# Blocks 14 and 15 of an interleaved down product, put back for two chunks of a four-layer prompt kernel

## The chip, the cores and the metric

The kernel runs on one core of a Trainium2 chip. The metric is the device time of one execution in microseconds (us). The engines are named as in the profile: PE is TensorE (PEld are its weight loads), DVE is VectorE, ACT is ScalarE, POOL is GpSimd, SP is SyncE, whose queue issues the transfers.

## The reference, cut to what matters

Two kinds of layers alternate, A, B, A, B, on x of 2048 tokens by 576 features. A is a dilated sliding-window attention (32 heads of 18 features, 8 keys at distance 0, 2, ... 14), B a gated product without an activation function. The same weights serve both A layers, and the same both B layers.

```python
x = x + A(layernorm(x), wqkv, wo)
x = x + B(layernorm(x), w_gate, w_up, w_down)
x = x + A(layernorm(x), wqkv, wo)
x = x + B(layernorm(x), w_gate, w_up, w_down)
...
def B(x, w_gate, w_up, w_down):   # w_gate, w_up: 576 x 4608, w_down: 4608 x 576
    h = (x @ w_gate) * (x @ w_up)
    return h @ w_down
```

The change lies in the last product, h @ w_down, of the first B layer.

## The kernel before, in words

**Tiles.** Tokens go in tiles of 128, so 2048 tokens are 16 tiles. The 4608 inner features of B are 36 feature tiles of 128 (`NFT`). The 576 outer features are four full row tiles and a tail of 64.

**Units and down blocks.** B is computed in units and blocks. A unit (`g_unit`, L1038) multiplies the normalised tokens with some feature tiles of w_gate and w_up into two PSUM banks: four full row tiles at L1046, the tail of 64 rows at L1056. Then ScalarE copies both banks out (L1000, L1002) and VectorE multiplies the two copies (L1003), which leaves h for these feature tiles in a buffer. Units are issued in batches (`batch`, L1014), so that the tails of several units run together. The down product (`Down`, L1065) accumulates h @ w_down over blocks. A block (`block`, L1091) takes `blk` feature tiles (2 here) for each token tile: for every pair of token tile and feature tile it loads h as weights and streams 512 columns of w_down (L1106), then loads it again for the last 64 columns (L1107). With 36 feature tiles there are 18 blocks. The first and last matmul of an accumulation are marked for the first and last block. `close` (L1118) adds the accumulators to the residual (L1123, L1133).

**Rows of w_down.** They come in pairs of feature tiles into a ring of six buffers wd (`load_wd`, L988). `fetch` (L1074) is called with each block and stays ahead of it by the length of the ring; it asks for all 18 pairs in order, whichever blocks are called.

**Stages.** The first 1024 tokens of the first B layer go through small stages, in which the weights are still arriving and attention of later chunks runs beside the matmuls: `first_pair` for two tiles, then `small` (L1240) three times for chunks of 256 tokens (entries 2, 3 and 4 of `seq`). Entry 2 runs all units and then all blocks. Entries 3 and 4, the third and fourth chunk, run with `inter` set: a unit has two feature tiles, there are 18 units (`nu`), and they share four buffers in hb in turn (`homes`, 14 + u % 4). So blocks must run between the units. In every second unit from u = 4 on, L1260 to L1262 run blocks u - 4 and u - 3, which read the units of these numbers. The loop ends at u = 17, so the last pair in it is blocks 12 and 13 at u = 16. The blocks left over come at L1265, behind the last batch (units 16 and 17). In the kernel before this second loop begins at `nu - 2` = 16, so blocks 14 and 15, feature tiles 28 to 31, are not added for these 512 tokens. After the small stages six large ones (`big`, L1270) take 512 tokens each, with units for one feature tile and 512 tokens.

**Order.** Every operation is recorded in a plan (`Plan`, L21) with a cost, its reads and writes, and a priority. `run` (L72) then issues greedily what can start first by its own clocks of the engines, the transfers and the free PSUM banks. Units and blocks hang on a chain in their own order (`bb`, L981); attention work (scores L744 to L754, softmax L785 to L852, values L912 and L928, output product L951, residual L957) and the transposes of the normalised input (L453, by transfers) are placed between them by the plan, some with a margin. Each engine runs its list in the order that the plan wrote, as does SP's queue.

Of the kernel before, what the change touches and what calls it, by code (L numbers as in the profile page):

```python
# [141 lines left out]
def kernel(  # L142
# [26 lines left out]
    NFT = F // P  # L169
# [347 lines left out]
    def place(la, t0, nst):  # L517
        b, o = order_sc.index((la, t0 // NSC)) % 2, t0 % NSC
        return xnT_B[b][:, :, o * P:(o + nst) * P], [f"xB{b}_{o + i}" for i in range(nst)]
# [518 lines left out]
    def g_unit(fts, xT, xk, n, dst, dk, act):  # L1038
        use, keys = [{}, {}], [f"{nm}_{dk}" for nm in ("wg", "wu")]

        def full(first, last_):
            for q, (nm, views) in enumerate((("wg", wgv), ("wu", wuv))):
                def fn(ws=[wcol(views, ft) for ft in fts], q=q):
                    for e, w_ in enumerate(ws):
                        for k in range(KF):
                            nc.tensor.matmul(ring[use[q]["slot"]][:, e * n:(e + 1) * n], lhsT=w_[:, k], rhs=xT[:, k],  # L1046
                                             start=(first and k == 0 and e == 0), stop=(last_ and k == KF - 1), skip_group_check=True)
                kw = dict(hold="ring", use=use[q]) if first else {}
                bb("PE", len(fts) * KF * (n / 2.4 + (1.8 if n < 256 else 2.9)), fn, r=xk + fkeys(nm, fts), w=[keys[q]], **kw)

        wt = [wcol(wtv, ft) for ft in fts]

        def tails(fresh):
            for e, w_ in enumerate(wt):
                for q, r_ in enumerate((slice(0, TL), slice(TL, 2 * TL))):
                    nc.tensor.matmul(ring[use[q]["slot"]][:, e * n:(e + 1) * n], lhsT=w_[r_], rhs=xT[r_, KF], start=(fresh and e == 0),  # L1056
                                     stop=not fresh, skip_group_check=True)

        def evac():
            fg, fu = [dict(free="ring", use=x) for x in use]  # L1060
            evacuate(lambda p_: ring[use[p_]["slot"]], keys, dst, dk, SC, act, fg, fu)
        return dict(use=use, keys=keys, full=full, tails=tails, npairs=len(fts), slotns=n * 0.42, evac=evac,
                    rk=xk + fkeys("wgt", fts) + fkeys("wut", fts), done=[])
# [82 lines left out]
    def pusher(size, opens=2):  # L1146
        bat = []

        def push(u=None, mid=None):
            if u is not None:  # L1150
                bat.append(u)
            if bat and (u is None or len(bat) == size):
                us = list(bat)
                bat.clear()
                batch(us, mid, opens)
        return push
# [9 lines left out]
    def hand_over(pool_k, slots):  # L1166
        for uses in slots:
            got, outs = {}, []

            def fn(got=got, outs=outs, uses=uses):  # L1170
                for p_, o_ in enumerate(outs):
                    o_.use["slot"] = 7 - got["slot"] if pool_k == "pa" else got["slot"] * uses + p_ + (4 if pool_k == "boot" else 0)
                    if pool_k == "boot" and o_.use["slot"] == 6:
                        o_.use["slot"], o_.free = 1, "pa"
            chain["pe"] = op("PE", 0, fn, prio=1, after=chain["pe"], hold=pool_k, use=got)
            for _ in range(uses):
                outs.append(op("PE", 0, lambda: None, prio=1, after=chain["pe"], free="ring", use={}))
                chain["pe"] = outs[-1]

    def begin_units(jobs, push):  # L1180
        for q in jobs:
            units = []
            begin(q, units)
            for x in units:
                push(x)

    def insert_d(jobs):
        for q in jobs:
            units = []
            begin(q, units)  # L1190
            while units:
                batch(units[:2])
                del units[:2]
# [46 lines left out]
    def small(j, inter, in_gu, in_d):  # L1240
        la, t0, nst = seq[j]
        n, fpu = nst * P, 4 // nst
        nu = NFT // fpu
        homes = [14 + u % 4 for u in range(nu)] if inter else [*range(9, 14), *range(9), *range(14, 18)]

        def lhs(ft, i):
            o = (ft % fpu) * n + i * P
            return hblk[homes[ft // fpu]][:, o:o + P]
        dn = Down(t0, nst, list(range(NFT)), lhs, lambda ft, i: f"hm{homes[ft // fpu]}", la == n_al - 1, False, 2)
        dn.fetch(len(wd_ring))  # L1250
        push = pusher(2, 1) if inter else pusher(3)
        marks["ld"], marks["ld1"] = marks.get("ld1"), chain["pe"]
        xT, xk = place(la, t0, nst)
        if j > 2:
            next(gens[j], None)
        if j == 3:
            hand_over("pa", (1,))
        for u in range(nu):
            begin_units(in_gu.get(u, ()), push)
            if inter and u % 2 == 0 and u > 2:  # L1260
                for b in (u - 4, u - 3):
                    dn.block(b)  # L1262
            push(g_unit(range(u * fpu, (u + 1) * fpu), xT, xk, n, hblk[homes[u]], f"hm{homes[u]}", True))
        push()
        for b in range(nu - 2 if inter else 0, NFT // 2):  # L1265
            insert_d(in_d.get(b, ()))
            dn.block(b)
        dn.close()
# [71 lines left out]
    for j in (2, 3, 4):  # L1340
        small(j, j > 2, IN_GU.get(j, {}), IN_D.get(j, {}))
# [38 lines left out]
```

## Time and profile before

| | |
|---|---|
| time, median of three runs | 1047.74 us |
| the three runs | 1047.56, 1047.74, 1049.56 us |
| the profiled execution, its own time | 1048.04 us |
| its span, first to last instruction | 1046.3 us |
| third chunk of 256 tokens: blocks 0 and 1 to blocks 16 and 17 | about 191 to 246 us |
| fourth chunk: the same | about 254 to 304 us |

The page gives busy time by engine, the span in slices, the chain that ended last, and groups of instructions by line; line numbers are those of the kernel before. A timeline row gives start, duration, engine, line, operation, output <- inputs, count, and in brackets the engine's idle time before it with the instruction that ended it. Matmuls overlap, since their recorded end is modelled; the distance of two starts is what one takes from the queue.

### The profile page before, as it was taken

The numbers are of one execution on the slowest core, as the hardware profiler recorded it, in microseconds if no ns is written. First come the engines' busy times: TensorE is split into PE (matmuls) and PEld (weight loads), VectorE is DVE, ScalarE is ACT, GpSimd is POOL, SyncE is SP. The second block draws the span as 40 slices with busy tenths as digits, with TensorE's granted clock in tenths as the row PEclk, the third lists the DMA queues.
The fourth block names the chain that finished last, engine by engine and source line by source line (L and its number), as shares of the span: only waits on it lengthen the run. The fifth ranks groups of instructions, "written<-read, shape, count | busy, mean of one in ns | idle before, by whom it ended". The sixth has DMA issues, their size and how long they took to land.

```text
span 1046.3 us, 19604 instructions
## 1 busy us (share of the span) xinstructions
PE 1028.7 (98%) x7898; PEld 598.7 (57%) x8016; DVE 723.7 (69%) x1366; ACT 446.3 (43%) x905; POOL 14.3 (1%) x54
## 2 busy tenths in 40 slices
PE   7999999999999999999999999999999999999998
PEld 6886886777765445554455544564455644554445
DVE  7896797879849886397776967579684696832211
ACT  5663763554645641354424443154431444214420
POOL 5000000000000000000000000000000000000000
PEclk9999999999999999999999999999999999999999
DMA  8928117445743705465143541625435252454212
GB/s 244 319 75 208 36 41 229 107 121 159 172 126 101 224 15 147 126 153 182 45 130 94 189 133 49 157 71 181 134 84 155 99 164 92 114 159 136 68 46 91
DMA packets 139850, 135.50 MB, mean 130 GB/s; under 512 B 43376, under 2 KB 137456, under 8 KB 139760
## 3 DMA queue, kind: packets, MB, share of 16 engines
q1 hardware_dynamic: 139760, 134.25, 44.2%
q8 instruction: 62, 1.02, 0.4%
q14 instruction: 28, 0.23, 0.1%
HBM read 114.49 MB, written 10.88 MB: 120 GB/s over the span
## 4 chain that ended last, share of the span: by engine, by line
PE 96%; issue 1%; DVE 1%; POOL 1%; DMA 1%; ACT 0%; POOLq 0%
PE pu L1046 20%; PE pg L1046 18%; PE pg L1106 8%; PE pu L1106 7%; PE acct L1046 6%; PE pg L551 5%; PE pa L1046 4%; PE pu L551 4%; PE acct L1106 3%; PE pu L1056 3%; PE pg L1056 3%; PE pg L1107 2%; PE pa L1106 2%; PE pu L1107 2%; PE pa L951 1%
## 5 line engine op out<-in xcount | busy, mean ns | idle before, releaser
L1046 PEld LDWEIGHTS <-reg 128*128 128x128 bf16 x3072 | 277.8, 98 | 222.3 <-issue 24.2
L1046 PE MATMUL pu<-xnT_B,reg 128*128 128x512 bf16 (+2 forms) x1302 | 231.4, 316 | 1.3 <-issue 0.3
L1046 PE MATMUL pg<-xnT_B,reg 128*128 128x512 bf16 (+2 forms) x1204 | 220.3, 319 | 1.0 <-issue 0.2
L1106 PEld LDWEIGHTS <-reg 128*128 128x128 bf16 x864 | 84.5, 98 | 98.2
L1000 ACT CAST g_sb<-pu 128x512 bf16<-128x512 f32 x112 | 65.6, 588 | 126.1 <-PE pg L1056 66.2
L1003 DVE TENSOR_TENSOR reg<-reg,g_sb 128x512 bf16<-128x512 bf16 x144 | 59.7, 419 | 86.0 <-ACT reg L1002 76.4
L551 PEld LDWEIGHTS <-wqkv 128*128 128x128 bf16 (+1 forms) x1050 | 88.2, 97 | 34.0 <-issue 18.2
L744 DVE TENSOR_TENSOR prod<-qT,kT 128x2560 bf16<-128x2560 bf16 (+1 forms) x68 | 96.4, 1420 | 8.2 <-ACT kT L671 7.1
L912 DVE TENSOR_TENSOR prod<-vT,ab 128x1280 bf16<-128x1280 bf16 (+1 forms) x120 | 92.1, 776 | 0.2 <-DMA ab<-a_dram 0.2
L1000 ACT CAST g_sb<-pg 128x512 bf16<-128x512 f32 x112 | 65.8, 589 | 60.8 <-PE pu L1056 30.1
L928 DVE TENSOR_TENSOR qT<-qT,prod 128x1280 bf16<-128x1280 bf16 (+1 forms) x112 | 89.7, 801 | 2.5
L1107 PEld LDWEIGHTS <-reg 128*128 128x128 bf16 x864 | 84.7, 98 | 1.8
L430 ACT ACTIVATE rstd<-mv,eps_t 128x2 f32<-128x2 f32 (+1 forms) x33 | 9.8, 297 | 162.8 <-DVE mv L426 159.9
L1046 PE MATMUL acct<-xnT_B,reg 128*128 128x512 bf16 (+1 forms) x303 | 69.4, 354 | 0.5 <-issue 0.3
L551 PE MATMUL pg<-xnT_A,wqkv 128*128 128x256 bf16 (+1 forms) x500 | 69.6, 273 | 0.0
L1056 PE MATMUL pu<-xnT_B,reg 64*128 64x512 bf16 (+2 forms) x331 | 67.6, 315 | 0.1
L1106 PE MATMUL pg<-wd,reg 128*128 128x512 bf16 (+1 forms) x232 | 63.9, 369 | 0.0
L1056 PE MATMUL pg<-xnT_B,reg 64*128 64x512 bf16 (+2 forms) x305 | 62.8, 318 | 0.0
L551 PE MATMUL pu<-xnT_A,wqkv 128*128 128x256 bf16 (+1 forms) x410 | 59.1, 273 | 0.1
L1106 PE MATMUL pu<-wd,reg 128*128 128x512 bf16 x200 | 54.8, 380 | 0.0
L1046 PE MATMUL pa<-xnT_B,reg 128*128 128x512 bf16 (+1 forms) x211 | 54.2, 375 | 0.6 <-issue 0.2
L1107 PE MATMUL pu<-wd,reg 128*128 128x64 bf16 x280 | 54.0, 193 | 0.8
(233 smaller groups left out, 1452.1 us busy)
## 6 DMA issues: line engine op xcount, KB each, us to landing
wd<-in_B_w_down_dram SPq DMA_DIRECT2D x152, 288.0 KB, 3.3
reg<-in_B_w_gate_dram SPq DMA_DIRECT2D x24, 768.0 KB, 4.7
reg<-in_B_w_up_dram SPq DMA_DIRECT2D x24, 768.0 KB, 6.3
reg<-in_B_w_down_dram SPq DMA_DIRECT2D x28, 288.0 KB, 3.3
s_dram<-s SPq DMA_DIRECT2D x13, 512.0 KB, 3.8
rg<-s_dram SPq DMA_DIRECT2D x52, 128.0 KB, 3.1
ab<-a_dram SPq DMA_DIRECT2D x52, 128.0 KB, 2.6
reg<-in_B_w_gate_dram SPq DMA_DIRECT2D x24, 96.0 KB, 5.4
```

Source lines behind the costliest of these rows:

```text
L430: nc.scalar.activation(rstd[:, 0:nst], mv[:, 0:nst, 1], ACT.Ln, bias=eps_t[:])
L551: nc.tensor.matmul(ring[use[p_]["slot"]][0:m, e * n:(e + 1) * n], lhsT=wqkv[r_, k, c0:c0 + m], rhs=xnT_A[r_, k, 0:n], start=start, stop=st ...
L744: nc.vector.tensor_tensor(late["prod"][lp(p_)][:, :, :, 0:n], q2, k2, op=ALU.mult)
L912: nc.vector.tensor_tensor(js(dst), js(vT[:, :, o0:o0 + n]), abw, op=ALU.mult)
L928: op("DVE", 60 + 3 * n, lambda tmp=tmp: nc.vector.tensor_tensor(oT[:, :, 0:n], oT[:, :, 0:n], tmp(), op=ALU.add), r=[pvk], w=ok, prio=prio)
L951: nc.tensor.matmul(b()[:, 0:HD], lhsT=oT[:, t, i * P:(i + 1) * P], rhs=wo_p[:, t, hh * HD:(hh + 1) * HD], start=(t == 0), stop=(t == KT - 1))
L1000: op("ACT", 590, lambda: nc.scalar.copy(g_sb[gs][:, 0:ul], bk(0)[:, 0:ul]), r=[keys[0]], w=[f"g{gs}"], prio=0, **fg)
L1003: op("DVE", 340, lambda: nc.vector.tensor_tensor(dst, dst, g_sb[gs][:, 0:ul], op=ALU.mult), r=[f"g{gs}"], w=[dk], prio=0)
L1046: nc.tensor.matmul(ring[use[q]["slot"]][:, e * n:(e + 1) * n], lhsT=w_[:, k], rhs=xT[:, k], start=(first and k == 0 and e == 0), stop=(las ...
L1056: nc.tensor.matmul(ring[use[q]["slot"]][:, e * n:(e + 1) * n], lhsT=w_[r_], rhs=xT[r_, KF], start=(fresh and e == 0), stop=not fresh, skip ...
L1106: nc.tensor.matmul(bank_of(i)[:, 0:cut], lhsT=lhs, rhs=wt[:, ft % 2, 0:cut], start=first and not plus, stop=last_)
L1107: nc.tensor.matmul(tail_of(i), lhsT=lhs, rhs=wt[:, ft % 2, cut:D], start=(first and not plus and (self.fin or i == 0)), stop=last_, skip_g ...
```

## The change

The second loop of `small` begins two blocks earlier where `inter` is set. Blocks 14 and 15 are then issued for the third and the fourth chunk, behind the batch of units 16 and 17 and ahead of blocks 16 and 17.

```diff
             push(g_unit(range(u * fpu, (u + 1) * fpu), xT, xk, n, hblk[homes[u]], f"hm{homes[u]}", True))
         push()
-        for b in range(nu - 2 if inter else 0, NFT // 2):
+        for b in range(nu - 4 if inter else 0, NFT // 2):
             insert_d(in_d.get(b, ()))
             dn.block(b)
         dn.close()
```

`insert_d` does nothing here, as `IN_D` (L1338) is empty. No other line is changed, but the plan orders all operations anew with the two blocks in it.

## The prediction

> **What bounds the kernel now.** I read the page first, then the waits of TensorE, then TensorE's timeline around the two chunks that the diff touches, then VectorE, ScalarE and SyncE in the same stretches.
>
> ```profile
> span 1046.3 us, 19604 instructions
> ...
> PE 1028.7 (98%) x7898; PEld 598.7 (57%) x8016; DVE 723.7 (69%) x1366; ACT 446.3 (43%) x905; POOL 14.3 (1%) x54
> ...
> PEclk9999999999999999999999999999999999999999
> ...
> PE 96%; issue 1%; DVE 1%; POOL 1%; DMA 1%; ACT 0%; POOLq 0%
> ```
>
> TensorE is busy in 98% of the span, its granted clock stands at the top digit in all 40 slices, and 96% of the chain that ended last is TensorE. A busy TensorE may still be an inefficient one, so the second view asks what it waited for.
>
> ```profile
> PE pu L599 <- POOL xf L307: 2.3, 1, 2.3
> PE acct L760 <- DVE prod L744: 2.1, 2, 1.9
> ...
> PE pu L1046 <- issue: 0.3, 2, 0.2
> ...
> PE pg L1106 <- DVE hb L1003: 0.2, 1, 0.2
> ```
>
> The columns are total, times and longest, in us. The two large waits belong to lines of the start-up (L599, L760), and behind them nothing is above 0.3 us. The last row is the one that counts here: the down product (L1106) waiting for a product in hb. After the start TensorE is an unbroken queue of matmuls, so a matmul put into it should move the end by its own issue interval, unless it stands where the queue had a gap.
>
> **What is added.** The weight loads of the down product show how much was left out.
>
> ```profile
> L1106 PEld LDWEIGHTS <-reg x864: 97/98/98, 390.3 to 1042.5; 128*128 128x128 bf16 x173
> ...
> L1106 PEld LDWEIGHTS <-hb x160: 95/98/98, 98.7 to 304.2; 128*128 128x128 bf16 x160
> ...
> L1106 PEld LDWEIGHTS <-xl x72: 97/98/98, 82.0 to 170.9; 128*128 128x128 bf16 x72
> ...
> L1106 PEld LDWEIGHTS <-xnT_B x40: 97/98/98, 88.4 to 159.7; 128*128 128x128 bf16 x40
> ```
>
> These sum to 1136. Sixteen token tiles in each of two layers with 36 feature tiles make 32 x 36 = 1152. Two blocks of two feature tiles for the two token tiles of each of two chunks are the missing 2 x 2 x 2 x 2 = 16. Each brings a 512-wide matmul (L1106), a 64-wide one (L1107) and a weight load for each: 32 matmuls and 32 loads of weights, which is also the difference between the two built programs on TensorE. No transfer is added: every call of the down product fetches all 18 pairs of wd rows, whether its blocks are read or not, and the page has 152 + 28 = 180 of them for ten calls.
>
> ```profile
> wd<-in_B_w_down_dram SPq DMA_DIRECT2D x152, 288.0 KB, 3.3
> ...
> reg<-in_B_w_down_dram SPq DMA_DIRECT2D x28, 288.0 KB, 3.3
> ```
>
> **What two blocks cost when nothing is late.** The next rows are TensorE's timeline in the third chunk (start, duration, instruction): first blocks 12 and 13, then blocks 16 and 17, which follow the last units of the chunk.
>
> ```profile
> 236.98 1.04 PE L1046 MATMUL pu<-xnT_B,reg 128*128 128x256 bf16 x8
> 237.86 0.38 PE L1106 MATMUL acct<-wd,hb 128*128 128x512 bf16 x1
> ...
> 239.08 0.38 PE L1106 MATMUL acct<-wd,hb 128*128 128x512 bf16 x1
> ...
> 239.33 0.38 PE L1106 MATMUL pg<-wd,hb 128*128 128x512 bf16 x1
> ...
> 239.82 1.04 PE L1046 MATMUL pu<-xnT_B,reg 128*128 128x256 bf16 x8
> ...
> 243.09 1.04 PE L1046 MATMUL pu<-xnT_B,reg 128*128 128x256 bf16 x8
> 244.01 0.39 PE L1106 MATMUL acct<-wd,hb 128*128 128x512 bf16 x1
> ...
> 245.26 0.39 PE L1106 MATMUL acct<-wd,hb 128*128 128x512 bf16 x1
> ...
> 246.25 1.04 PE L1046 MATMUL pu<-xnT_B,reg 128*128 128x256 bf16 x8
> ```
>
> The recorded 0.38 us of a matmul overlaps the next one, so I go by starts. From 239.08 to 239.33 a pair of 512 and 64 columns takes 0.245 us. Blocks 12 and 13, eight pairs, run from 237.86 to 239.82: 1.96 us. Two chunks: 2 x 1.96 = **3.92 us** of queue.
>
> The Trainium skill, "TensorE: Matmul & The Clock Gate", section Part 3: Packing small matmuls, under The mechanism, has a rule that speaks against this price: a weight load overlaps running matmuls only where its row group differs, and here all loads use all rows. By that rule the pair would show both loads, and the change would cost nearly twice as much (second rival below). This trace disagrees: the load for the 64-wide matmul starts at 239.08, as the 512-wide one does.
>
> ```profile
> 239.08 0.10 PEld L1107 LDWEIGHTS <-hb 128*128 128x128 bf16 x1
> ```
>
> **What the added blocks cover.** Blocks 16 and 17 of the third chunk took 246.25 - 244.01 = 2.24 us for the same eight pairs, 0.28 above 1.96. The excess sits before block 17, where the start due at 244.01 + 4 x 0.245 = 244.99 came at 245.26. Another 0.04 lies ahead of block 16: from the last eight matmuls of the unit it started 244.01 - 243.09 = 0.92 us later, against 237.86 - 236.98 = 0.88. The fourth chunk has the same place:
>
> ```profile
> 301.29 1.04 PE L1046 MATMUL pu<-xnT_B,reg 128*128 128x256 bf16 x8
> 302.16 0.38 PE L1106 MATMUL pg<-wd,hb 128*128 128x512 bf16 x1
> ...
> 303.46 0.39 PE L1106 MATMUL pg<-wd,hb 128*128 128x512 bf16 x1 [0.16 <-DVE hb L1003]
> ...
> 304.45 0.60 PE L551 MATMUL pu<-xnT_A,wqkv 128*128 128x256 bf16 x4
> ```
>
> Here it is 304.45 - 302.16 = 2.29 us, 0.33 above. VectorE shows why: these blocks read the last two units' products as they come.
>
> ```profile
> 243.54 0.42 DVE L1003 TENSOR_TENSOR hb<-hb,g_sb 128x512 bf16<-128x512 bf16 x1
> ...
> 244.78 0.42 DVE L1003 TENSOR_TENSOR hb<-hb,g_sb 128x512 bf16<-128x512 bf16 x1
> ...
> 246.72 0.68 DVE L1123 TENSOR_TENSOR xf<-acct,xf 128x512 bf16<-128x512 f32 x1
> ```
>
> The products are written at 243.96 and 245.20, just ahead of the late starts at 244.01 and 245.26. With blocks 14 and 15 in between (their own inputs come from the units before, long written), block 16 starts 1.96 us later and both products are there. So the added blocks buy back 0.04 + 0.28 + 0.33 = **0.65 us**. If none came back the term would be 0; more than 0.65 it cannot be, as no larger gap is there.
>
> **What moves beside them.** The planner orders everything anew, and the built programs tell how. On TensorE, apart from the insertions, only output products (L951) move against their neighbours in the fourth chunk, and once, around 413 us, four pairs of L1106/L1107 change places with L951 groups; no count changes. The first L951 group moves from 262.11 to just ahead of the matmuls that start at 258.88; it reads the attention output that VectorE finished with the L928 below.
>
> ```profile
> 258.88 1.92 PE L1046 MATMUL pu<-xnT_B,reg 128*128 128x256 bf16 x16
> 260.64 0.38 PE L1106 MATMUL pg<-wd,hb 128*128 128x512 bf16 x1
> ...
> 262.11 0.78 PE L951 MATMUL pa<-wo_p,qT 128*128 128x288 bf16 x5
> ...
> 285.20 0.28 PE L1056 MATMUL acct<-xnT_B,reg 64*128 64x256 bf16 x1
> ```
> ```profile
> 256.21 0.42 DVE L793 TENSOR_TENSOR rg<-Lt 128x256 f32<-128x256 f32 x1
> ...
> 258.45 0.82 DVE L912 TENSOR_TENSOR prod<-vT,ab 128x1280 bf16<-128x1280 bf16 x1
> 259.30 0.82 DVE L928 TENSOR_TENSOR qT<-qT,prod 128x1280 bf16<-128x1280 bf16 x1
> ...
> 282.56 0.82 DVE L928 TENSOR_TENSOR qT<-qT,prod 128x1280 bf16<-128x1280 bf16 x1
> ```
>
> On TensorE that place now comes at 258.88 + 1.96 - 0.32 = 260.52. On VectorE the last L912/L928 pair moves ahead of the softmax's second half (L793 on), so it ends about 258.45 - 256.21 = 2.24 us earlier than 260.12, plus at most the same shift of 1.64: 259.5. The group is 1.0 us in time. The softmax behind it ends later by that pair, 1.6 us, and with it the next chain, whose last L928 ended at 283.38; its first L951 goes ahead of the tails at 285.20, that is 286.84 with the shift, and 283.38 + 1.6 leaves 1.9 us. The accumulators of the two chunks are emptied by L1123, 0.47 us behind the last block now; the shift carries both along. Cost of all moves: 0, and 1.24 if this cover is gone (first rival).
>
> On SyncE's queue the loads that refill the two wd buffers of blocks 14 and 15 now wait for these blocks, and are put behind the attention's gathers. Their data is next read by blocks 2 and 3 of the next chunk; those started at 260.64 and will at 262.3, some 16 us behind the end of blocks 14 and 15 near 246, against 3.3 us for a landing. The transposes of the next layer's input also shift in that queue:
>
> ```profile
> 298.72 2.54 SPq L453 DMA_TRANSPOSE xnT_B<-xn  x2
> ```
>
> They now stand in part behind wd loads that wait for blocks 12 and 13. Those end ahead of the row at 301.29 above, so the transposes go out before 301.29 + 1.64 = 302.9; the large stage that reads them lies behind the row at 304.45, which moves to 307.7. Cost 0.
>
> **The sum.** 3.92 - 0.65 = +3.27 us. The profiled execution took 1048.04 us with its span of 1046.3, so its like would take 1051.3. It lay 0.30 above the median of the runs shown, so against that median: 1047.74 + 3.27 = **1051.0 us**, +0.31%.
>
> **Rivals.** (1) *A new wait at the moved L951.* If VectorE's last pair keeps its old end and shifts whole with TensorE, it ends at 260.12 + 1.64 = 261.76, and the group at 260.52 waits 1.24 us, with the whole queue behind it. Against it stands VectorE's new order; for it, that VectorE is the busiest engine beside TensorE there. Time: 1047.74 + 3.27 + 1.24 = 1052.3.
>
> (2) *Weight loads in the open.* If the two loads of 98 ns stood in series with each pair, 16 pairs would cost 16 x (0.245 + 0.196) = 7.06 us, and 1047.74 + 7.06 - 0.65 = 1054.2. This is the rule of the Trainium skill cited above. Against it: every neighbouring block shows 0.245.
>
> (3) *Not slower: the added queue runs into a wait that stays where it is.* Where TensorE next waits for a transfer with a time of its own, a later arrival costs nothing. The place would be the change to the large stage, whose inputs are the transposes above. It decides from an absorbed 3.27 - 2.1 = 1.2 us on; with all absorbed the time is 1047.7. Against it: no wait of TensorE behind the start is longer than 0.3 us, so at most about that can be absorbed at one place.
>
> (4) *The change does nothing*, the planner dropping the blocks: 1047.7. The new program's 16 more L1106 exclude it, all but mishaps.
>
> **How the numbers follow.** Forecast 0.82, rival 1 0.10, rival 2 0.02, rival 3 0.05, rival 4 0.01. A change below 0.2%, 2.1 us, is not told from none here. Forecast and rivals 1 and 2 are slower by more: 0.94, less 0.02 for a forecast that lands low because a median of few runs moves (those shown reach from 1047.56 to 1049.56): slower 0.92. Rivals 3 and 4 are "same", with that 0.02, less 0.01 for faster: same 0.07, faster 0.01. The forecast's own bounds are 3.27 and, with nothing bought back, 3.92, so 1051.0 to 1051.7; the median's scatter of some 1 us lowers the bottom to 1049.9, and rival 1 with that scatter's smaller part sets the top at 1053.0.
>
> **What would show it.** In the changed kernel's timeline four more pairs per block stand ahead of blocks 16 and 17 in both chunks, at 0.245 us each; blocks 16 and 17 take 1.96 us; the row with L1106 waiting for hb L1003 is gone from TensorE's waits; the row now at 304.45 starts at 307.7; behind it every start is later by the same 3.3. I am wrong if TensorE's waits have a new row of a us (L951 for L928, or L1046 for a transpose), if a pair takes other than 0.245, or if the shift at 308 is not the shift at the end.

## The result and the profile after

The changed kernel takes 1052.38 us (median of 6 runs, 1050.63 to 1053.26), the kernel before 1047.87 us beside it (6 runs, 1047.56 to 1049.56). The ratio is 1.0038 with an interval of 1.0025 to 1.0051. The profiled execution took 1052.47 us. One execution of the kernel before, of 1794.3 us at a granted clock of 0.557, is left out of all comparisons below.

The head of the page, kernel after:

```profile
span 1050.6 us, 19667 instructions
...
PE 1031.9 (98%) x7929; PEld 600.5 (57%) x8048; DVE 725.7 (69%) x1366; ACT 446.8 (43%) x905; POOL 14.6 (1%) x54
...
PEclk9999999999999999999999999999999999999999
...
PE 96%; DVE 1%; issue 1%; DMA 1%; SPq 0%; ACT 0%
```

TensorE has 32 more loads of weights (8048 against 8016) and 3.2 us more busy time (31 more matmuls: the records of matmuls are not complete). No other engine has another count. Its waits, kernel after (total, times, longest, in us):

```profile
PE acct L760 <- DVE prod L744: 3.2, 4, 1.6
PE pa L967 <- POOL ident L316: 1.4, 1, 1.4
PE pg L599 <- ACT xnT_A L463: 1.3, 1, 1.3
...
PE pu L1046 <- issue: 0.6, 4, 0.2
```

The waits above half a us are those of the start-up and of issue. The row with L1106 waiting for the product in hb is gone, and no L951 or L1046 waits for data. TensorE's timeline at the end of the third chunk, kernel after: the last matmuls of the last unit, then the first matmul of block 14, of block 16 and of block 17, then the next unit.

```profile
243.93 1.04 PE L1046 MATMUL pu<-xnT_B,reg 128*128 128x256 bf16 x8
244.80 0.38 PE L1106 MATMUL acct<-wd,hb 128*128 128x512 bf16 x1
...
246.76 0.38 PE L1106 MATMUL acct<-wd,hb 128*128 128x512 bf16 x1
...
247.74 0.38 PE L1106 MATMUL acct<-wd,hb 128*128 128x512 bf16 x1
...
248.72 1.04 PE L1046 MATMUL pu<-xnT_B,reg 128*128 128x256 bf16 x8
```

The same place in the fourth chunk, kernel after:

```profile
303.76 1.04 PE L1046 MATMUL pu<-xnT_B,reg 128*128 128x256 bf16 x8
304.63 0.38 PE L1106 MATMUL pg<-wd,hb 128*128 128x512 bf16 x1
...
306.59 0.38 PE L1106 MATMUL pg<-wd,hb 128*128 128x512 bf16 x1
...
308.55 0.60 PE L551 MATMUL pu<-xnT_A,wqkv 128*128 128x256 bf16 x4
```

Blocks 14 and 15 take 1.96 us in both chunks, and blocks 16 and 17 now take 1.96 us too (246.76 to 248.72 and 306.59 to 308.55). From the last matmuls of the unit to what follows the blocks it is 4.79 us in both chunks; before it was 246.25 - 243.09 = 3.16 and 304.45 - 301.29 = 3.16. So each chunk gained 1.63 us, together 3.26.

The row at 304.45 now starts at 308.55, however, 4.10 later and not 3.26. To see where the other 0.84 came from, I split the execution at two instructions that both programs have: the first L1106 of the third chunk and the first L551 behind the fourth. The windows between them, and from there to just ahead of the last matmul, of before (columns: stretch, length, busy time of PE, PEld, DVE, ACT and POOL with counts, granted clock, DMA share, GB/s):

```profile
191.48:304.45 112.97, 111.88 (x1012) 81.50 (x1026) 88.03 (x173) 55.94 (x112) 0.00 (x0) 1.00 0.56 145
304.45:1042.70 738.25, 732.69 (x4699) 372.62 (x4790) 481.73 (x891) 281.72 (x566) 0.00 (x0) 1.00 0.40 119
```

and of after:

```profile
192.32:308.55 116.23, 115.39 (x1045) 83.61 (x1058) 88.04 (x173) 55.48 (x112) 0.00 (x0) 1.00 0.54 139
308.55:1046.80 738.25, 732.15 (x4698) 372.60 (x4790) 482.22 (x891) 282.43 (x566) 0.00 (x0) 1.00 0.40 120
```

The stretch with the two chunks is 116.23 - 112.97 = 3.26 us longer. What follows it is as long as in the kernel before: the last matmul starts at 1042.75 before and at 1046.85 after, 738.30 behind the end of the stretch in both. The 0.84 us stand ahead of the stretch, which began at 192.32 instead of 191.48, in code that the change does not touch: up to the begin both traces show the same instructions in the same order on every engine, and as many (107) of the start-up's fill matmuls of L967.

### The profile page after: what moved, and what is told of

Same layout as the page of the kernel before. It is cut to its first block, busy times and chain, and to the rows that moved or that the text cites. A ratio compares the mean times of both kernels' runs of the same rounds, so it can differ in the third digit from the quotient of the medians.

```text
span 1050.6 us, 19667 instructions
## 1 busy us (share of the span) xinstructions
PE 1031.9 (98%) x7929; PEld 600.5 (57%) x8048; DVE 725.7 (69%) x1366; ACT 446.8 (43%) x905; POOL 14.6 (1%) x54
## 4 chain that ended last, share of the span: by engine, by line
PE 96%; DVE 1%; issue 1%; DMA 1%; SPq 0%; ACT 0%
PE pg L1046 19%; PE pu L1046 19%; PE pu L1106 9%; PE pg L1106 7%; PE acct L1046 6%; PE pu L551 5%; PE pa L1046 4%; PE pg L551 4%; PE acct L1106 3%; PE pg L1056 3%; PE pu L1056 2%; PE pg L1107 2%; PE pa L1106 2%; PE pu L1107 1%; PE pa L951 1%
## 5 line engine op out<-in xcount | busy, mean ns | idle before, releaser
L1046 PEld LDWEIGHTS <-reg 128*128 128x128 bf16 x3072 | 277.8, 98 | 222.3 <-issue 24.2
L1046 PE MATMUL pg<-xnT_B,reg 128*128 128x512 bf16 (+2 forms) x1234 | 226.4, 321 | 1.2 <-issue 0.2
L1046 PE MATMUL pu<-xnT_B,reg 128*128 128x512 bf16 (+2 forms) x1269 | 223.6, 314 | 1.4 <-issue 0.6
L1106 PEld LDWEIGHTS <-reg 128*128 128x128 bf16 x864 | 84.5, 98 | 98.2
L551 PEld LDWEIGHTS <-wqkv 128*128 128x128 bf16 (+1 forms) x1050 | 88.2, 97 | 34.0 <-issue 18.2
L928 DVE TENSOR_TENSOR qT<-qT,prod 128x1280 bf16<-128x1280 bf16 (+1 forms) x112 | 89.7, 801 | 2.5
L551 PE MATMUL pu<-xnT_A,wqkv 128*128 128x256 bf16 (+1 forms) x520 | 73.6, 273 | 0.1
L1056 PE MATMUL pg<-xnT_B,reg 64*128 64x512 bf16 (+2 forms) x314 | 69.9, 321 | 0.6
L1046 PE MATMUL acct<-xnT_B,reg 128*128 128x512 bf16 (+1 forms) x297 | 68.9, 354 | 0.6 <-issue 0.2
L1106 PE MATMUL pu<-wd,reg 128*128 128x512 bf16 x251 | 69.1, 380 | 0.0
L1107 PE MATMUL pg<-wd,reg 128*128 128x64 bf16 x348 | 67.1, 193 | 0.9
L1056 PE MATMUL pu<-xnT_B,reg 64*128 64x512 bf16 (+2 forms) x322 | 60.3, 313 | 0.1
L551 PE MATMUL pg<-xnT_A,wqkv 128*128 128x256 bf16 (+1 forms) x390 | 58.5, 273 | 0.0
L1046 PE MATMUL pa<-xnT_B,reg 128*128 128x512 bf16 (+1 forms) x215 | 55.1, 375 | 0.2
L1056 PEld LDWEIGHTS <-reg 64*128 64x128 bf16 x768 | 29.9, 94 | 36.2 <-issue 24.2
```

Of the source, the lines that this page charges most:

```text
L551: nc.tensor.matmul(ring[use[p_]["slot"]][0:m, e * n:(e + 1) * n], lhsT=wqkv[r_, k, c0:c0 + m], rhs=xnT_A[r_, k, 0:n], start=start, stop=st ...
L928: op("DVE", 60 + 3 * n, lambda tmp=tmp: nc.vector.tensor_tensor(oT[:, :, 0:n], oT[:, :, 0:n], tmp(), op=ALU.add), r=[pvk], w=ok, prio=prio)
L1106: nc.tensor.matmul(bank_of(i)[:, 0:cut], lhsT=lhs, rhs=wt[:, ft % 2, 0:cut], start=first and not plus, stop=last_)
L1107: nc.tensor.matmul(tail_of(i), lhsT=lhs, rhs=wt[:, ft % 2, cut:D], start=(first and not plus and (self.fin or i == 0)), stop=last_, skip_g ...
```

## The experiments

Two things were open. Are the terms of the 3.26 us what the prediction takes them for, 0.245 us for each pair of matmuls and 0.65 us bought back? And is the later begin of the stretch an effect of the change, which would make the true price 4.1 us, or scatter of what lies ahead of it? "Begin", "stretch" and "rest" below are the windows above, the rest taken to the start of the last matmul.

| kernel | begin | stretch | rest | profiled time | median (runs) | ratio, interval |
|---|---|---|---|---|---|---|
| before | 191.48 | 112.97 | 738.30 | 1048.04 | 1047.87 (6) | |
| after | 192.32 | 116.23 | 738.30 | 1052.47 | 1052.38 (6) | 1.0038, 1.0025 to 1.0051 |
| after, again | 192.22 | 116.23 | 738.30 | 1052.27 | 1052.14 (6) | 1.0032, 1.0018 to 1.0046 |
| block 15 alone | 192.91 | 114.27 | 738.30 | 1050.79 | 1049.26 (11) | 1.0008, 0.9999 to 1.0016 |
| blocks inside the loop | 191.25 | 117.21 | 738.30 | 1052.32 | 1052.93 (6) | 1.0041, 1.0025 to 1.0057 |
| before, again | 191.94 | 112.97 | 738.30 | 1048.49 | 1048.49 (11) | 1.0005, 0.9995 to 1.0015 |
| blocks added twice | 191.66 | 120.14 | 738.31 | 1055.62 | 1055.70 (4) | 1.0060, 1.0046 to 1.0074 |
| more fill at the start | 194.24 | 116.23 | 738.30 | 1054.29 | 1054.00 (5) | 1.0042, 1.0028 to 1.0056 |
| before, third time | 190.79 | 112.97 | 738.30 | 1047.36 | 1048.40 (11) | 0.9997, 0.9988 to 1.0006 |
| after, third time | 190.78 | 116.22 | 738.30 | 1050.82 | 1051.66 (7) | 1.0031, 1.0020 to 1.0042 |

**Both kernels again, unedited.** The changed kernel:

> The changed kernel once more, nothing edited. In the first profiles the stage from the first L1106 of the third chunk to the first L551 behind the fourth grew from 112.97 us (191.48 to 304.45) to 116.2, that is by 3.27; the start of that stage lay 0.84 us later, all of it from before 36 us. Theory (3.27 us of queue, and a start-up that scatters from execution to execution for reasons of its own): the stage is again 116.2, its start anywhere between 191 and 193. Rival (the changed program starts later by itself, some 0.8 us each time): its start is again near 192.3 while the kernel before, profiled again, is again near 191.5, and the median stays 4 us above the kernel before.

The kernel before:

> The kernel before once more, nothing edited; blocks 14 and 15 of the third and fourth chunk are left out. Theory: stage 112.97 us again, its start scattered as in the changed kernel. Rival (a start-up that belongs to the program): its start within 0.2 us of 191.48.

The stretch is the same to 0.01 us in each; only the begin moves, 192.22 and 191.94. For the changed kernel the rival of its expectation had a begin near 192.3 too, so these two profiles do not decide the second question; the third ones below do.

**Block 15 alone.** Block 14 stays out:

```diff
-        for b in range(nu - 4 if inter else 0, NFT // 2):
+        for b in range(nu - 3 if inter else 0, NFT // 2):
```

> Only block 15 is put back in the two chunks; block 14 (feature tiles 28 and 29) is left out. Theory (a block costs 0.98 us of queue and any cover of more than 0.33 us buys back the whole 0.65 us of waits): the stage is 112.97 + 2 x 0.98 - 0.65 = 114.28 us, and the time 1.3 us above the kernel before. Rival (the waits are bought back in proportion to the blocks, or what was bought back is chance): 112.97 + 1.96 - 0.33 = 114.6, or with nothing bought back 114.93.

TensorE's timeline in the third chunk, block 15 alone:

```profile
244.52 1.04 PE L1046 MATMUL pu<-xnT_B,reg 128*128 128x256 bf16 x8
245.39 0.38 PE L1106 MATMUL acct<-wd,hb 128*128 128x512 bf16 x1
...
248.33 1.04 PE L1046 MATMUL pu<-xnT_B,reg 128*128 128x256 bf16 x8
```

Three blocks take 248.33 - 245.39 = 2.94 us, 0.98 each, and start 0.87 behind the unit's matmuls. The stretch is 114.27 us, 1.30 above that of before: 2 x 0.98 of queue less the whole 0.65. So one block (0.98 us of cover) is enough to hide the late products, and the second block is pure queue. The times alone would not show it: their ratio is 1.0008 with an interval that reaches below 1.

**The blocks added twice.** Blocks 14 and 15 run two times in each of the two chunks, so their products are added twice there:

```diff
-        for b in range(nu - 4 if inter else 0, NFT // 2):
+        for b in [nu - 4, nu - 3, *range(nu - 4, NFT // 2)] if inter else range(NFT // 2):
```

> Blocks 14 and 15 are issued twice in both chunks, so their part is added twice; nothing else differs from the changed kernel. Theory (a block of eight matmuls costs 0.98 us of queue, no more and no less, once the late products are covered): the stage is 116.22 + 4 x 0.98 = 120.14 us, the time 3.9 us above the changed kernel. Rival (the added blocks also delay other engines, so that a cost beyond the queue grows with them): above 120.14 by a new wait.

The two ends of the stretch in this kernel, in TensorE's timeline:

```profile
191.66 0.38 PE L1106 MATMUL acct<-wd,hb 128*128 128x512 bf16 x1
...
311.80 0.60 PE L551 MATMUL pa<-xnT_A,wqkv 128*128 128x256 bf16 x4
```

The stretch is 311.80 - 191.66 = 120.14 us, 3.91 above that of after. With nothing left to buy back, 16 pairs cost 16 x 0.245 = 3.92.

**The blocks inside the loop.** The kernel before, with blocks 14 and 15 in the step of blocks 12 and 13 at u = 16, ahead of the last batch. The same work is added, but nothing stands between units 16 and 17 and the blocks that read them:

```diff
-                for b in (u - 4, u - 3):
+                for b in (u - 4, u - 3, *((nu - 4, nu - 3) if u == nu - 2 else ())):
```

> Blocks 14 and 15 are put back, but behind blocks 12 and 13, ahead of the last batch of units, so that nothing covers the last two products. Theory: the same 3.92 us of queue, and blocks 16 and 17 again take about 2.24 and 2.29 us; the stage is 112.97 + 3.92 = 116.89 us, 0.65 longer than in the changed kernel, the time 3.9 us above the kernel before. Rival (the place does not matter, the late products have other reasons): 116.2 as in the changed kernel. A new wait of block 14 for the product of unit 14 or 15 would show as a stage above 116.9.

TensorE's timeline at the end of the third chunk, blocks inside the loop:

```profile
244.82 1.04 PE L1046 MATMUL pu<-xnT_B,reg 128*128 128x256 bf16 x8
246.24 0.39 PE L1106 MATMUL acct<-wd,hb 128*128 128x512 bf16 x1 [0.39 <-DMA rg<-s_dram]
...
248.30 1.04 PE L1046 MATMUL pu<-xnT_B,reg 128*128 128x256 bf16 x8
...
306.17 0.38 PE L1106 MATMUL pg<-wd,hb 128*128 128x512 bf16 x1
...
307.47 0.39 PE L1106 MATMUL pg<-wd,hb 128*128 128x512 bf16 x1 [0.16 <-DVE hb L1003]
...
308.46 0.60 PE L551 MATMUL pu<-xnT_A,wqkv 128*128 128x256 bf16 x4
```

In the fourth chunk blocks 16 and 17 take 2.29 us (306.17 to 308.46) as they did before the change: the 0.33 is back. In the third chunk block 16 was due 0.87 behind 244.82, at 245.69, and came at 246.24, 0.55 late; the two blocks then take 2.06, 0.10 above 1.96. Together 0.55 + 0.10 + 0.33 = 0.98, and 112.97 - 0.65 + 3.92 + 0.98 = 117.22 against the measured 117.21. That is 0.32 above what was expected of it, since the third chunk lost 0.65 and not its old 0.32. VectorE's and ScalarE's timelines there, blocks inside the loop, show the reason:

```profile
245.03 0.82 DVE L928 TENSOR_TENSOR qT<-qT,prod 128x1280 bf16<-128x1280 bf16 x1
245.77 0.42 DVE L1003 TENSOR_TENSOR hb<-hb,g_sb 128x512 bf16<-128x512 bf16 x1
...
246.84 0.42 DVE L1003 TENSOR_TENSOR hb<-hb,g_sb 128x512 bf16<-128x512 bf16 x1
```
```profile
244.30 0.59 ACT L1002 CAST hb<-pg 128x512 bf16<-128x512 f32 x1
```

The plan now puts the product of unit 16 behind three more operations of the attention, the last of them the L928 above. The copy that the product reads was done at 244.89, but the product started at 245.77 only. It ends at 245.77 + 0.42 = 246.19, and block 16 starts at 246.24. The bracket of the 246.24 row names a transfer into rg, which this matmul does not read: releasers are inferred, and the timeline of the engine that writes the input corrects it. So the 0.65 is no constant: what cover is worth depends on where the plan puts the last products, here 0.98.

**More fill at the start.** The changed kernel's start-up contains matmuls that only keep the clock up; here 198 of them instead of 107:

```diff
-            self.warm(min(44, int(max(0, t - clock["PE"] - 100) / 100)))
+            self.warm(min(80, int(max(0, t - clock["PE"] - 100) / 56)))
```

> The changed kernel with the start-up's gaps on TensorE filled more densely by matmuls of no use (one per 56 ns of planned gap instead of one per 100, at most 80 at a place): 198 of them instead of 107, all before the first unit of B; the rest is the same. Profiles so far show a granted clock of one half for 3.4 to 6.8 us between 15 and 22 us, in one execution not at all, and the begin of the stage between 191.25 and 192.91 us. Theory A (this clock is what scatters the start-up): no stretch at half clock, the begin of the stage at or below 191.3 and the time 0.5 to 1.5 us below the changed kernel. Theory B (the scatter comes from transfers and VectorE, and TensorE's clock there hides behind them): begin of the stage within the old range, time unchanged within 0.5 us. The stage itself stays 116.22 us in both.

The reason to look there is the clock between 12 and 24 us. The windows of after, the second a part of the first, and of the kernel with more fill:

```profile
12.00:24.00 12.00, 8.81 (x175) 7.47 (x174) 10.70 (x23) 6.66 (x12) 3.75 (x7) 0.86 0.98 281
...
20.00:22.00 2.00, 2.00 (x17) 1.42 (x16) 1.24 (x4) 1.34 (x4) 0.00 (x0) 0.50 1.05 323
```
```profile
12.00:24.00 12.00, 10.96 (x243) 9.64 (x241) 9.84 (x23) 6.66 (x12) 3.80 (x16) 1.00 0.92 270
```

Over 12 to 24 us the granted clock is 0.86 in the changed kernel (0.14 x 12 / 0.5 = 3.4 us at half clock, with the 0.50 of the second row) and 1.00 in the kernel with more fill. Yet that one begins the stretch at 194.24, the latest of all, so neither theory of the expectation came out. Two rows of its TensorE timeline hold a good part of the delay:

```profile
38.53 0.21 PE L1056 MATMUL pg<-xnT_B,reg 64*128 64x128 bf16 x1 [1.44 <-issue]
...
164.87 0.38 PE L1106 MATMUL pg<-wd,xl 128*128 128x512 bf16 x1 [0.69 <-DMA wd<-in_B_w_down_dram]
```

For 1.44 us TensorE waited for nothing that the profile shows, and for 0.69 us for rows of w_down. So a full clock at the start is not enough for an early begin. Whether a lower clock has a share in a late one this run cannot tell, since the 91 added matmuls stand in the start-up themselves.

**Both kernels a third time.** The kernel before:

> The kernel before, third profile; blocks 14 and 15 of the two chunks are left out. So far the begin of the stage lay at 191.48 and 191.94 us for this program, at 192.32 and 192.22 for the changed one, between 191.25 and 192.91 for its variants. Theory (scatter that belongs to the execution): stage 112.97 us, begin anywhere from 191 to 193, times between 1047 and 1051. Rival (the changed program begins its stage later by some 0.5 us or more of its own): begin below 192 again.

The changed kernel:

> The changed kernel, third profile. Theory: stage 116.22 us, begin anywhere from 191 to 193 us, so that over all executions of both programs the times differ by 3.3 us within 0.5. Rival: begin above 192.2 a third time and the times of all executions 3.8 us or more above those of the kernel before.

Windows of the kernel before, third time, and of the changed one, third time:

```profile
12.00:24.00 12.00, 10.12 (x209) 8.44 (x208) 11.06 (x25) 7.37 (x15) 2.92 (x6) 0.86 0.90 269
```
```profile
12.00:24.00 12.00, 9.18 (x202) 7.66 (x203) 11.53 (x26) 7.84 (x15) 2.56 (x5) 1.00 0.91 271
```

Begins of 190.79 and 190.78, one with and one without the stretch at half clock. Over the three executions of each kernel the begins are 191.48, 191.94 and 190.79 before, and 192.32, 192.22 and 190.78 after: a later begin does not come with the change. The times say the same. Mean of all runs after less mean of all runs before, within each of the three sets of runs that hold both kernels: 4.02 with a 95% interval of 0.94 to either side, 3.33 with 0.81, 3.28 with 0.63; weighted by these, 3.46 with 0.44. The 3.27 of the sum lies within all of them, and 4.1 as the true price does not lie within the weighted one.

## Why the prediction came out as it did

**The queue price, 3.92 us: held.** Blocks 14 and 15 take 1.96 us in each chunk, block 15 alone 0.98, and doubling the blocks adds 3.91 once more. TensorE has no slack there into which a matmul could go.

**Bought back, 0.65 us: held, and shown by taking it away.** With the blocks in their new place the products are written long before they are read: VectorE's rows, kernel after,

```profile
244.38 0.42 DVE L1003 TENSOR_TENSOR hb<-hb,g_sb 128x512 bf16<-128x512 bf16 x1
...
245.62 0.42 DVE L1003 TENSOR_TENSOR hb<-hb,g_sb 128x512 bf16<-128x512 bf16 x1
```

end at 244.80 and 246.04, and blocks 16 and 17 start at 246.76 and 247.74. With the same work inside the loop the waits are there again, and larger.

**The moves, 0: held.** TensorE's and VectorE's rows of the moved output product, kernel after:

```profile
261.35 0.79 PE L951 MATMUL pa<-wo_p,qT 128*128 128x288 bf16 x5
```
```profile
258.17 0.82 DVE L928 TENSOR_TENSOR qT<-qT,prod 128x1280 bf16<-128x1280 bf16 x1
258.90 0.42 DVE L793 TENSOR_TENSOR rg<-Lt 128x256 f32<-128x256 f32 x1
```

L951 starts at 261.35, that is the forecast 260.52 with the 0.84 of the start-up. The last L928 ends at 258.99, ahead of L793 as VectorE's new order had it, 2.4 us before it is needed. So rival 1, a new wait of 1.24 us at this place, is out. The transposes also came in time; SyncE's queue, kernel after:

```profile
297.54 1.21 SPq L453 DMA_TRANSPOSE xnT_B<-xn  x1
...
301.14 1.21 SPq L453 DMA_TRANSPOSE xnT_B<-xn  x1
```

Both go out ahead of 302.9, the bound of the forecast, and nothing waits for them.

**Rivals 2, 3 and 4.** Weight loads in series would have made the stretch 7.06 - 0.65 = 6.41 us longer; it was 3.26. The line of the Trainium skill behind that rival ("TensorE: Matmul & The Clock Gate", Part 3: Packing small matmuls, The mechanism: a weight load overlaps running matmuls only where its row group differs) does not describe this trace, in which every added pair, with two loads over all rows, takes 0.245 us in four kernels. A wait that absorbs the shift (rival 3) is excluded by the rest of 738.30 us, and rival 4, a change without effect, by the 32 loads.

**Where it was off.** The step that failed is the last check of the prediction, that the row at 304.45 would start at 307.7 and the shift there be the change's own 3.3 us. It took the begin of the stretch as given. In the first execution of each kernel the begin differed by 0.84 us, for no cause found in the change, so the row came at 308.55 and the profiled time at 1052.47 where 1051.3 was forecast for its like. The sum itself, +3.27 against 3.26 measured in the stretch, was right. What sets the begin in one execution stays open; where it arises is shown in the last section.

**Where it was lucky.** The first median, 1052.38, lies 1.4 us above the forecast of 1051.0 and above 1051.7, the forecast's own upper bound. It is inside the stated range only because the top, 1053.0, made room for rival 1, which did not occur: the prediction used the scatter of some 1 us for the bottom, but the begin also scatters upwards. By the time alone rival 1, with its 1052.3, would have looked like the better account; only the timeline tells the two apart. The later runs (1052.14 and 1051.66) came nearer to the forecast.

**Two readings that were too short.** Behind the two large waits of before stand two more of the start-up, among the rows that the prediction leaves out: L967 for 1.4 and 0.8 us. And the top digit of the clock in all 40 slices, of 26 us each, hides a stretch at a lower clock: over 12 to 24 us the kernel before was granted 0.86. Neither enters the sum.

## What to carry to other kernels

Where TensorE is an unbroken queue, the price of an added matmul is its distance of starts in a neighbouring block, and the discount found here is a gap that it fills; look for the late producer behind each such gap, and place added work between producer and reader rather than ahead of both. Where one such effect is smaller than the scatter of the times, measure between two instructions that both programs share: here that repeats to 0.01 us, where the times of one kernel scatter over 3 us. Before a shift at the end is put down to the change, see where it arises. And a time inside the range does not show that the forecast mechanism made it: here a rival that did not occur was nearer.

## What the hardware showed beside it

What scatters lies ahead of the stretch. Unedited programs, with the same start-up code, begin it between 190.78 and 192.32 us, and the remaining 738.30 us then repeat to 0.01 us in all ten profiled executions. Two places can be told apart by the start of the first L1106 of the program, near 82 us, and its distance to the begin. "Wait" is what TensorE's waits list for L1106 and rows of w_down in between, "clock" the granted clock over 12 to 24 us.

| kernel | clock | first L1106 | from there to the begin | wait |
|---|---|---|---|---|
| before | 0.86 | 82.04 | 109.45 | |
| after | 0.86 | 82.87 | 109.45 | |
| after, again | 0.72 | 82.59 | 109.63 | |
| block 15 alone | 0.86 | 82.59 | 110.32 | 0.8 |
| blocks inside the loop | 0.86 | 82.02 | 109.23 | |
| before, again | 1.00 | 81.76 | 110.18 | 0.8 |
| blocks added twice | 0.86 | 82.43 | 109.23 | |
| more fill at the start | 1.00 | 84.16 | 110.08 | 0.7 |
| before, third time | 0.86 | 81.49 | 109.30 | |
| after, third time | 1.00 | 81.02 | 109.75 | 0.4 |

The first place is the start-up: with the same start-up code the first L1106 comes between 81.02 and 82.87 us. The 0.84 us of the first two profiles are all from there, since the distance is 109.45 in both. The stretch at half clock falls in other places from one execution to the next: the same two matmuls of L863 took, in TensorE's timeline of before and of after,

```profile
20.88 0.38 PE L863 MATMUL pu<-a_c,Bsel 128*128 128x256 bf16 x2
```
```profile
21.25 0.63 PE L863 MATMUL pu<-a_c,Bsel 128*128 128x256 bf16 x2
```

0.38 and 0.63 us. The two executions at full clock with the same start-up code are the first and the third by their first L1106 (81.02 and 81.76), but those at 0.86 spread from 81.49 to 82.87. A share of the clock is possible and not shown.

The second place is a wait for rows of w_down: without a listed wait the distance is 109.23 to 109.63, with one 109.75 to 110.32. The chain that ended last has, before and with block 15 alone,

```profile
169.44 5.44 DMA wd<-in_B_w_down_dram
```
```profile
169.99 6.32 DMA wd<-in_B_w_down_dram
```

the same step of TensorE's queue behind a pair of rows of w_down, 0.88 us longer in the second, whose begin of 192.91 is the latest but for the kernel with more fill. Why these lengths vary, and what the 1.44 us without a releaser are, was not settled.
